# Two MLP pairs by whole products, token sums over both, and decoding that runs ahead and then rests

## The chip, the cores and the metric

The program runs on one core of a Trainium2 chip. The metric is the device time of one execution in microseconds (us); the time of before is the median of three runs. A core has TensorE (PE, the matrix products), VectorE (DVE), ScalarE (ACT), GpSimd (POOL) and SyncE (SP, which issues the transfers). Each takes its own instructions strictly in order; they wait for one another by semaphores.

## The reference, cut to what matters

```python
attn_out = attention(q, k, v, omega)          # linear attention over random features
x = attn_out.transpose(0, 2, 1, 3).reshape(2304, 512)
rms = sqrt(mean(x * x) + 1e-6);  xn = x / rms * rms_g
g = xn @ w_gate;  val = xn @ w_val            # GLU: 512 -> 1536
x = (g * sigmoid(g) * val) @ w_out            # 1536 -> 512
h = x @ w_in                                  # MLP: 512 -> 2048
out = (h * sigmoid(h)) @ w_out2               # 2048 -> 512
```

The weights are doubles (64 bit) in memory.

## The kernel before, in words

Attention comes first and fills about 180 us. The rest, of which the change is a part, is a stream of products over five blocks of tokens (0 to 3 of 512 tokens, 4 of 256). Each number is kept as a high and a low half (`xs` for tokens, `h` for hidden values, `w` for weights), and a product of two numbers is three matmuls (`PASS`, L191): 12 matmuls of 512 columns for one 128-wide slice of hidden features over one block (`part`, L205, or `product`, L513).

**GLU sweeps.** `groups` holds nine GLU groups of one slice (u = 0 to 8), then eight MLP groups of two slices each, a "pair" (u = 9 to 16). The first pair is `u == std` (9). Every group but `std` goes through `quad` (L520): blocks 0 and 1 against two weight matrices by seven half products of six matmuls in place of eight, which needs sums of token halves (`token_sums`, L344, L318 on POOL, halves by L327 and L330) and sums of weight halves (`sum12`, `sum34`, `shi`, `slo`). `std` alone uses whole products for blocks 0 and 1 (`g1_mlp`), since the token sums of the MLP's input don't exist yet. Blocks 2 to 4 are whole products everywhere.

**Second products.** `g2_glu` (L259) and `g2_mlp` (L292) multiply the hidden values by the output weights, tile by tile of 512 columns (a "y tile"), into one of four PSUM buffers `y`. In GLU sweeps DVE adds each tile to `ya` (L270); the buffer is free after that. Block 4's own first products use the same ring of four buffers. In the last GLU sweep (`done`) the sum is also the MLP's input: ACT writes its high half (L272) and DVE the low half (L249) into `xs`. So after the last sweep's first products come, in PE's order, y tiles of blocks 0 to 4 mixed with first products of blocks 3 and 4 and of `std` over blocks 0 and 1. This stretch is called the passage here.

**Decoding.** Every weight matrix comes as raw doubles by one transfer of SP, is decoded by five DVE operations (L146 to L157) and two POOL additions (L160), and split by ACT (high half, L411) and DVE (low half, L415). `WeightQueue` holds this as a list of jobs in a fixed order; each says how many free weight buffers it needs. The loop at the end of the kernel (L1484 to L1491) walks the stream, adds up the PE time of each piece in `due`, and lets one job be emitted whenever `due` exceeds `M_PACE` (2.0), unless `wq.hold` is set, as it is inside `quad`. A product that needs a weight emits the jobs up to it at once (`need`). Steps of the token sums (`sums`) are emitted by the same loop, one for each `T_PACE` (1.2) of PE time. The place at which a step is emitted is its place in its engine's order.

Of the kernel before, what the change touches and what calls it, by code (L numbers as in the profile page):

```python
# [20 lines left out]
def kernel(  # L21
# [168 lines left out]

    PASS = [(0, 0), (0, 1), (1, 0)]  # L191
    HALVES = [slice(0, 64), slice(64, P)]
    M_PACE, T_PACE = 2.0, 1.2
    W_EARLY, GRAIN, GATE = 3, 3, 3

    def split_h(s, j):
# [111 lines left out]

    KH = KC // 2
    tok, sums, ready = {}, [], set()  # L310
    std = next(u for u, g in enumerate(groups) if g[0] == 2)

    def w_tile(side, slot, dtype=F32R):
# [52 lines left out]

    class WeightQueue:
        def __init__(self):
            self.jobs, self.st, self.hold, self.free, self.held, self.tail = [], {}, True, [], {}, []
            for u in range(len(groups)):  # L370
                self.plan(u)

# [23 lines left out]
        def plan(self, u):  # L396
# [47 lines left out]
            load = self.load  # L444
            if kind == 1:
                jobs = [
                    (0, lambda: dec(a1, 1), lambda: load(u + 1, 1, 1)),
                    *self.tail,
                    (0, lambda: dec(a0, 0), lambda: load(u, bs[0], 0)),
# [8 lines left out]
                    (0, lambda: slo(1)),  # L458
                ]
                self.tail = [(1, lambda: hi(bs[0])), (0, lambda: lo(bs[0]))]  # L460
            elif u == std:
                jobs = [
                    *self.tail,
                    (0, lambda: dec(a1, 1), lambda: load(u, bs[1], 1)),
                    (0, lambda: dec(a0, 0), lambda: load(u, bs[0], 0)),
                    (0,),
                    (1, lambda: hi(a1)),
                    (1, lambda: lo(a1), lambda: hi(a0)),
                    (0, lambda: lo(a0), lambda: dec(bs[0], 0), lambda: load(u + 1, 0, 0)),
                    (0, lambda: dec(bs[1], 1), lambda: load(u + 1, 1, 1)),  # L470
                    (0,),
                    (1, lambda: hi(bs[0])),
                    (1, lambda: lo(bs[0]), lambda: hi(bs[1])),
                    (0, lambda: lo(bs[1])),
                ]
            else:
                jobs = [
                    (0, lambda: dec(a0, 0)),
                    (0, lambda: dec(a1, 1), lambda: load(u, bs[0], 0)),
                    (1, lambda: hi(a0), lambda: load(u, bs[1], 1)),  # L480
                    (1, lambda: lo(a0), lambda: hi(a1)),
                    (0, lambda: lo(a1), sum12),
                    (0, sum34),
                    (1, lambda: shi(0)),
                    (0, lambda: slo(0)),
                    (1, lambda: shi(1), lambda: dec(bs[0], 0)),
                    (0, lambda: slo(1), lambda: load(u + 1, 0, 0)),
                    (1, lambda: hi(bs[0]), lambda: dec(bs[1], 1)),
                    (0, lambda: lo(bs[0]), lambda: load(u + 1, 1, 1)),
                    (1, lambda: hi(bs[1])),  # L490
                    (0, lambda: lo(bs[1])),
                ]
# [143 lines left out]
    def stream():  # L636
# [25 lines left out]
        for u, (kind, fs) in enumerate(groups):  # L662
            first, last = kind == 2 and fs[0] == 0, u == len(groups) - 1
            done = u + 1 == std
            hs = {j: {} for j in range(NB)}
            if u == std:
                out_of = lambda j: g2_mlp(fs, j, hs[j], True, False, False)
                ys = iter(pend)
                now, later = token_sums(
                    lambda k: w_tile(1, 7, F32) if k == 2 else wq.slot(("t", k), F32),  # L670
                    lambda n: wq.release(("t", 1 - n)),
                )
                yield from g1_mlp(fs[0], 0, hs[0], (), take(ys, 4))
                yield from g1_mlp(fs[1], 0, hs[0], (), take(ys, 4))
                sums.extend(now)
                yield from g1_mlp(fs[0], 1, hs[1], (), ys)
                wq.release(*wq.keys(u - 1)[1])
                yield from g1_mlp(fs[1], 1, hs[1], (), out_of(0))
                sums.extend(later)
                yield from g1_mlp(fs[0], 2, hs[2], (), out_of(1))  # L680
                yield from g1_mlp(fs[1], 2, hs[2], (), ())
            else:
                yield from quad(u, iter(pend), hs)
            if u == std:
                pass
            elif u:
                wq.release(*wq.keys(u - 1)[1])
            else:
                wq.free += spent
# [9 lines left out]
                wq.release(*wq.keys(u)[0])  # L699
            else:  # L700
                out_of = lambda j, end=False: g2_mlp(fs, j, hs[j], first, last, end)
                if u != std:
                    for n, f in enumerate(fs):
                        yield from g1_mlp(f, 2, hs[2], (), out_of(1 - n))
                if last:
# [709 lines left out]
    with tc.manual_schedule():  # L1415
# [50 lines left out]
        n = 0  # L1466
# [13 lines left out]
        pools["w"][1] = late  # L1480
        pools["h"] = (late, 4)
        pools["s"] = (late, 3)
        due = 0.0
        for c in stream():  # L1484
            due += c
            if sums and due > T_PACE:
                sums.pop(0)()
                if wq.hold:
                    due = 0.0
            if due > M_PACE and not wq.hold and (wq.tick() or sums):  # L1490
                due = min(due - M_PACE, M_PACE)  # L1491


# [28 lines left out]
```

## Time and profile before

| | |
|---|---|
| median of 3 runs | 984.78 us (983.47 to 986.15) |
| profiled execution | 984.44 us, its span 982.7 us |
| PE busy | 949.7 us, 97% of the span |
| DVE, ACT, POOL busy | 699.1, 433.6, 416.5 us |
| mean granted TensorE clock | 0.991 of full speed |

Busy time of PE is of matmuls that overlap each other, so it reads as full wherever matmuls follow each other without a gap. The profile's slices show it full in nearly every slice; what it isn't full in lies at the start, near 220 us, and between 550 and 625 us. The last of these is the passage.

### The profile page before, as it was taken

Reading aid. Unit: us, or ns where it says so; the run is one execution under the profiler, and the core shown is the slowest. Engines: PE = TensorE matmul, PEld = TensorE weight load, DVE = VectorE, ACT = ScalarE, POOL = GpSimd, SP = SyncE. Lnnn points to the kernel's source line nnn. Section 1 sums busy time; section 2 is a strip of 40 time slices with the busy share of each in tenths; the row PEclk is TensorE's granted clock in tenths of the full one; section 3 lists DMA queues with packets and bytes.
Section 4 is the critical chain, followed back from the end, with each engine's and each line's share of the span. In section 5 each row is a group of like instructions: output and inputs, shape, how many; then the busy total and the mean of one; then the engine's idle time right before and its main releaser. Section 6 shows DMA issues by size and latency. Waiting matters only on the chain.

```text
span 982.7 us, 17038 instructions
## 1 busy us (share of the span) xinstructions
PE 949.7 (97%) x6564; PEld 794.2 (81%) x6564; DVE 699.1 (71%) x1372; ACT 433.6 (44%) x983; POOL 416.5 (42%) x406
## 2 busy tenths in 40 slices
PE   8999999998999999999999777999999999999998
PEld 6888878877888888888888655888888888888887
DVE  6998999656677677776767787648576757676653
ACT  6999886523433333333333234543242333333321
POOL 8887744315435335435533533324243333424200
PEclk9999999999999999999999989999999999999999
DMA  7654543012111112012011220002020211111023
GB/s 192 164 144 126 140 128 89 1 43 65 43 43 44 44 43 64 23 43 65 25 42 42 65 65 0 24 22 85 13 74 22 65 32 54 44 44 43 1 75 118
DMA packets 79489, 60.42 MB, mean 61 GB/s; under 512 B 27312, under 2 KB 73648, under 8 KB 79408
## 3 DMA queue, kind: packets, MB, share of 16 engines
q1 hardware_dynamic: 79136, 59.26, 20.8%
q8 instruction: 52, 0.85, 0.4%
q14 instruction: 29, 0.24, 0.1%
q10 hardware_dynamic: 272, 0.07, 0.0%
HBM read 49.87 MB, written 4.72 MB: 56 GB/s over the span
## 4 chain that ended last, share of the span: by engine, by line
PE 86%; DVE 7%; ACT 2%; DMA 2%; POOL 2%; issue 1%; SPq 1%; DVEq 0%; POOLq 0%
PE g L205 20%; PE y L292 20%; PE g L513 16%; PE y L259 12%; PE y L205 5%; PE b L992 3%; PE b L205 2%; PE b L1392 2%; PE kv L1072 2%; PE b L1176 2%; PE b L965 1%; DVE xs L249 1%; DVE ya L270 1%; POOL m L160 1%; PE b L1152 1%
## 5 line engine op out<-in xcount | busy, mean ns | idle before, releaser
L160 POOL TENSOR_TENSOR m<-m,raw 128x512 int32<-128x512 int32 x136 | 204.9, 1509 | 341.2 <-issue 193.5
L205 PE MATMUL g<-xs,w 128*128 128x512 f32 x1008 | 245.9, 391 | 0.0
L205 PEld LDWEIGHTS g<-xs,w 128*128 128x128 f32 x1008 | 189.9, 189 | 39.4
L292 PE MATMUL y<-w,h 128*128 128x512 f32 (+1 forms) x870 | 209.1, 390 | 3.9 <-ACT h L198 2.8
L292 PEld LDWEIGHTS y<-w,h 128*128 128x128 f32 x870 | 163.4, 189 | 38.9 <-ACT h L198 3.2
L259 PE MATMUL y<-h,w 128*128 128x512 f32 (+1 forms) x648 | 158.7, 371 | 15.2 <-DVE ya L270 9.8
L199 DVE TENSOR_TENSOR h<-s,h 128x512 fp32r<-128x512 f32 (+1 forms) x134 | 101.1, 759 | 95.0 <-ACT h L198 94.2
L270 DVE TENSOR_TENSOR ya<-y,ya 128x512 f32<-128x512 f32 (+1 forms) x200 | 123.0, 631 | 34.4 <-PE y L259 34.3
L259 PEld LDWEIGHTS y<-h,w 128*128 128x128 f32 x648 | 114.2, 190 | 38.4 <-DVE ya L270 10.4
L303 DVE TENSOR_TENSOR ya<-y,ya 128x512 f32<-128x512 f32 (+1 forms) x127 | 84.3, 679 | 56.9 <-PE y L292 56.3
L198 ACT ACTIVATE h<-s 128x512 fp32r<-128x512 f32 (+1 forms) x134 | 77.0, 585 | 100.6 <-DVE s L616 46.6
L513 PE MATMUL g<-xs,w 128*128 128x512 f32 x384 | 97.8, 390 | 0.0
L411 ACT ACTIVATE w<-m 128x512 fp32r<-128x512 f32 x75 | 47.1, 628 | 86.5 <-POOL m L160 73.9
L513 PEld LDWEIGHTS g<-xs,w 128*128 128x128 f32 x384 | 71.5, 188 | 14.8
L1041 ACT ACTIVATE e<-b,nb 128x128 f32<-128x128 f32 x272 | 76.1, 425 | 7.5 <-issue 4.3
L415 DVE TENSOR_TENSOR w<-m,w 128x512 fp32r<-128x512 f32 x66 | 59.6, 902 | 22.6 <-ACT w L411 22.6
L513 PE MATMUL g<-w,w 128*128 128x512 f32 x288 | 73.3, 390 | 0.0
L205 PEld LDWEIGHTS y<-xs,w 128*128 128x128 f32 x480 | 61.6, 191 | 8.2 <-DVE ya L270 6.1
L205 PE MATMUL y<-xs,w 128*128 128x256 f32 x480 | 62.7, 283 | 5.2 <-DVE ya L270 5.2
L513 PEld LDWEIGHTS g<-w,w 128*128 128x128 f32 x288 | 53.5, 188 | 10.7
L1009 DVE TENSOR_REDUCE small<-b 128x4 f32<-128x512 f32 (+1 forms) x80 | 51.3, 642 | 6.4 <-PE b L992 2.9
L536 ACT ACTIVATE s<-s 128x512 f32<-128x512 f32 x23 | 14.5, 632 | 80.1 <-DVE s L541 80.1
(119 smaller groups left out, 1165.2 us busy)
## 6 DMA issues: line engine op xcount, KB each, us to landing
raw<-in_moe_w_out_dram SPq DMA_DIRECT2D x28, 512.0 KB, 3.6
raw<-in_moe_w_in_dram SPq DMA_DIRECT2D x16, 512.0 KB, 3.6
raw<-in_moe_w_gate_dram SPq DMA_DIRECT2D x12, 512.0 KB, 3.5
raw<-in_moe_w_val_dram SPq DMA_DIRECT2D x12, 512.0 KB, 3.5
qT<-e SPq DMA_DIRECT2D x72, 64.0 KB, 2.3
x<-in_k_dram SPq DMA_DIRECT2D x16, 256.0 KB, 3.5
x<-in_q_dram SPq DMA_DIRECT2D x16, 256.0 KB, 3.0
va<-in_v_dram SPq DMA_DIRECT2D x32, 128.0 KB, 3.9
```

What stands on the lines that cost most here:

```text
L160: tt(out=mi, in0=mi, in1=(low if step == 5 else high).bitcast(I32), op=ALU.add)
L198: nc.scalar.activation(out=ht[:, 0, :], in_=s, func=AF.Copy)
L199: nc.vector.tensor_tensor(out=ht[:, 1, :], in0=s, in1=ht[:, 0, :].bitcast(F32), op=ALU.subtract)
L205: nc.tensor.matmul(out=ps, lhsT=w[:, a, cc * P:(cc + 1) * P], rhs=xs[j][:, c, cc, :], start=(n == 0), stop=(n == 3 * KC - 1),)
L259: nc.tensor.matmul(out=ps, lhsT=wt[1, "o", f][:, a, d * P:(d + 1) * P], rhs=hs[f][:, c, :], start=(n == 0), stop=(n == nn - 1),)
L270: nc.vector.tensor_tensor(out=y[:, d, :], in0=ps, in1=y[:, d, :], op=ALU.add)
L292: nc.tensor.matmul(out=ps, lhsT=hs[f][:, a, t * P:(t + 1) * P], rhs=wt[2, "p", f][:, c, d0:d1], start=(n == 0), stop=(n == nn - 1),)
L303: nc.vector.tensor_tensor(out=o[:, t, d0:d1], in0=ps, in1=o[:, t, d0:d1], op=ALU.add)
L415: eng.tensor_tensor(out=v[:, 1, :], in0=x, in1=v[:, 0, :].bitcast(F32), op=ALU.subtract)
L513: nc.tensor.matmul(out=ps, lhsT=w[:, a, (c0 + c) * P:(c0 + c + 1) * P], rhs=x(b, c), start=(start and n == 0), stop=(n == 3 * KH - 1), ski ...
L1009: nc.vector.tensor_reduce(out=st.mx.rearrange("p (j e) -> p e j", e=2)[:, e], in_=st.ps[e], axis=AX.X, op=ALU.max)
L1041: nc.scalar.activation(out=st.e[r][:, :, h, :] if blocks4 else st.e[r][:, h, :], in_=src.rearrange("p (a f) -> p a f", a=4) if blocks4 els ...
```

## The change

Four things change.

1. The first two pairs (`NSTD = 2`, u = 9 and 10) use whole products for blocks 0 and 1. The jobs of both have no weight sums any more.
2. The token sums start after `std`'s four products over blocks 0 and 1 (before: after the two over block 0), and their last two steps come in the second pair. A new counter `gone` spaces them: `T_PACE` while decoding rests, `M_PACE + T_PACE` otherwise.
3. In the last four GLU sweeps (u = 5 to 8) a job is emitted for every `A_PACE` = 1.6 of PE time and not 2.0. The first sweep gets one empty job ahead.
4. At the start of `std` `wq.hold` is set, and cleared after its fourth product over blocks 0 and 1 and the y tiles of block 0. While it is set, `due` is capped at `M_PACE`.

```diff
-    M_PACE, T_PACE = 2.0, 1.2
+    M_PACE, A_PACE, T_PACE = 2.0, 1.6, 1.2
...
+    NSTD = 2
...
             if kind == 1:
                 jobs = [
+                    *[(0,)] * (u == 0),
...
-            elif u == std:
+            elif std <= u < std + NSTD:
                 jobs = [
+                    (0, lambda: dec(a1, 1), lambda: load(u, bs[1], 1)),
                     *self.tail,
-                    (0, lambda: dec(a1, 1), lambda: load(u, bs[1], 1)),
                     (0, lambda: dec(a0, 0), lambda: load(u, bs[0], 0)),
-                    (0,),
                     (1, lambda: hi(a1)),
-                    (1, lambda: lo(a1), lambda: hi(a0)),
-                    (0, lambda: lo(a0), lambda: dec(bs[0], 0), lambda: load(u + 1, 0, 0)),
+                    (0, lambda: lo(a1)),
                     (0, lambda: dec(bs[1], 1), lambda: load(u + 1, 1, 1)),
+                    (1, lambda: hi(a0)),
+                    (0, lambda: lo(a0)),
+                    (0, lambda: dec(bs[0], 0), lambda: load(u + 1, 0, 0)),
...
+            wq.pace = A_PACE if std - 4 <= u < std else M_PACE
             hs = {j: {} for j in range(NB)}
-            if u == std:
+            if std <= u < std + NSTD:
...
+                wq.hold = first
                 yield from g1_mlp(fs[0], 0, hs[0], (), take(ys, 4))
                 yield from g1_mlp(fs[1], 0, hs[0], (), take(ys, 4))
-                sums.extend(now)
                 yield from g1_mlp(fs[0], 1, hs[1], (), ys)
                 wq.release(*wq.keys(u - 1)[1])
                 yield from g1_mlp(fs[1], 1, hs[1], (), out_of(0))
-                sums.extend(later)
+                wq.hold = False
+                if first:
...
+                    sums.extend(now)
+                if u == std + NSTD - 1:
+                    sums.extend(later)
                 yield from g1_mlp(fs[0], 2, hs[2], (), out_of(1))
...
-        due = 0.0
+        due = gone = 0.0
         for c in stream():
             due += c
-            if sums and due > T_PACE:
+            gone += c
+            if sums and gone > (T_PACE if wq.hold else M_PACE + T_PACE):
                 sums.pop(0)()
-                if wq.hold:
-                    due = 0.0
-            if due > M_PACE and not wq.hold and (wq.tick() or sums):
-                due = min(due - M_PACE, M_PACE)
+                gone = 0.0
+            if wq.hold:
+                due = min(due, M_PACE)
+            elif due > wq.pace and wq.tick():
+                due = min(due - wq.pace, wq.pace)
```

Three places show what moves. Names: `ya_95` to `ya_97`, `ya_3689` and `ya_3690` are the sums of blocks 0 to 4, `xs_90` to `xs_94` the tokens of blocks 0 to 4; line numbers after L310 are higher by one to five in the changed kernel.

First, DVE at the head of the passage, from the last `h` of the quad to the first y tile of block 0. Before:

```order
L146 TENSOR_SCALAR m_6849<-raw_6434 128x512
L149 TENSOR_SCALAR raw_6434<-raw_6434 128x512
L152 TENSOR_SCALAR m_6849<-m_6849 128x512
L154 TENSOR_SCALAR raw_6434<-raw_6434 128x512
L157 TENSOR_SCALAR m_6849<-m_6849 128x512
L146 TENSOR_SCALAR m_6860<-raw_6659 128x512
L149 TENSOR_SCALAR raw_6659<-raw_6659 128x512
L152 TENSOR_SCALAR m_6860<-m_6860 128x512
L154 TENSOR_SCALAR raw_6659<-raw_6659 128x512
L157 TENSOR_SCALAR m_6860<-m_6860 128x512
L270 TENSOR_TENSOR ya_95<-y,ya_95 128x512
```

The same place now, one row further on:

```order
L146 TENSOR_SCALAR m_6885<-raw_6685 128x512
L149 TENSOR_SCALAR raw_6685<-raw_6685 128x512
L152 TENSOR_SCALAR m_6885<-m_6885 128x512
L154 TENSOR_SCALAR raw_6685<-raw_6685 128x512
L157 TENSOR_SCALAR m_6885<-m_6885 128x512
L416 TENSOR_TENSOR w_0_6896<-m_6726,w_0_6896 128x512
L270 TENSOR_TENSOR ya_95<-y,ya_95 128x512
L621 TENSOR_TENSOR s<-s,g 128x512
L270 TENSOR_TENSOR ya_95<-y,ya_95 128x512
L249 TENSOR_TENSOR xs_90<-ya_95,xs_90 128x512
L416 TENSOR_TENSOR w_3_6926<-m_6885,w_3_6926 128x512
```

Two decodings stood ahead of the first L270 of `ya_95`; now one does, and the low half of a weight decoded earlier (L416). Further on, two decodings stand between the y tiles of block 0 in both kernels.

Second, DVE in the middle of the passage, from the last low half of block 1's tokens (`xs_91`) to the y tiles of block 2. Before:

```order
L249 TENSOR_TENSOR xs_91<-ya_96,xs_91 128x512
L146 TENSOR_SCALAR m_7054<-raw_6929 128x512
L149 TENSOR_SCALAR raw_6929<-raw_6929 128x512
L152 TENSOR_SCALAR m_7054<-m_7054 128x512
L154 TENSOR_SCALAR raw_6929<-raw_6929 128x512
L157 TENSOR_SCALAR m_7054<-m_7054 128x512
L270 TENSOR_TENSOR ya_97<-y,ya_97 128x512
L146 TENSOR_SCALAR m_7080<-raw_6952 128x512
L149 TENSOR_SCALAR raw_6952<-raw_6952 128x512
L152 TENSOR_SCALAR m_7080<-m_7080 128x512
L154 TENSOR_SCALAR raw_6952<-raw_6952 128x512
L157 TENSOR_SCALAR m_7080<-m_7080 128x512
```

The same place now:

```order
L249 TENSOR_TENSOR xs_91<-ya_96,xs_91 128x512
L199 TENSOR_TENSOR h<-s,h 128x256
L249 TENSOR_TENSOR xs_91<-ya_96,xs_91 128x512
L270 TENSOR_TENSOR ya_97<-y,ya_97 128x512 x2
L249 TENSOR_TENSOR xs_92<-ya_97,xs_92 128x512
L270 TENSOR_TENSOR ya_97<-y,ya_97 128x512
L249 TENSOR_TENSOR xs_92<-ya_97,xs_92 128x512
L270 TENSOR_TENSOR ya_97<-y,ya_97 128x512
L249 TENSOR_TENSOR xs_92<-ya_97,xs_92 128x512
L199 TENSOR_TENSOR h<-s,h 128x512
L249 TENSOR_TENSOR xs_92<-ya_97,xs_92 128x512
L270 TENSOR_TENSOR ya_3689<-y,ya_3689 128x512 x2
```

Both decodings are gone from here. One of them now stands between the y tiles of block 1, the others come after the passage.

Third, ACT behind the passage, after the last high half of block 4's tokens. Before:

```order
L239 ACTIVATE s<-g 128x512
L198 ACTIVATE h<-s 128x512
L411 ACTIVATE w_1_7228<-ws 128x512
L301 ACTIVATE ya_95<-y 128x512 x4
L327 ACTIVATE w_5_7279<-w_1_7174 128x1024
L239 ACTIVATE s<-g 128x512
L198 ACTIVATE h<-s 128x512
```

The same place now:

```order
L239 ACTIVATE s<-g 128x512
L198 ACTIVATE h<-s 128x512
L301 ACTIVATE ya_95<-y 128x512 x4
L239 ACTIVATE s<-g 128x512
L198 ACTIVATE h<-s 128x512
L301 ACTIVATE ya_96<-y 128x512
L412 ACTIVATE w_5_7310<-m_7026 128x512
L301 ACTIVATE ya_96<-y 128x512 x3
L239 ACTIVATE s<-g 128x512
L198 ACTIVATE h<-s 128x512
```

The high half of a token sum (L327 on `w_1`, which POOL makes) stood ahead of a silu (L239) and a high half of `h` (L198); now none stands there, and the four L327 come one by one from the start of the second pair on. On PE the second pair's seven groups of six matmuls over blocks 0 and 1 become four groups of twelve.

## Rows read from the trace of the kernel before

**Rows 1.** Windows of 25 us: PE, PEld, DVE, ACT, POOL busy; clock; DMA.

```profile
475.00:500.00 25.00, 25.00 (x123) 21.17 (x122) 18.21 (x35) 8.18 (x17) 14.41 (x12) 1.00 0.20 62
...
550.00:575.00 25.00, 16.68 (x75) 13.61 (x74) 21.37 (x33) 9.12 (x17) 9.24 (x7) 0.86 0.27 84
```

**Rows 2.** Lines of PE from 545.8 to 636.1, shapes apart: busy, mean | idle before.

```profile
L205 PE MATMUL g<-xs,w 128*128 128x512 f32 x127 | 32.8, 406 | 0.0
L292 PE MATMUL y<-w,h 128*128 128x512 f32 x72 | 19.1, 420 | 3.9 <-ACT h L198 2.8 <-DVE ya L270 1.1
L259 PE MATMUL y<-h,w 128*128 128x512 f32 x48 | 14.1, 414 | 6.6 <-DVE ya L270 6.6
L205 PE MATMUL y<-xs,w 128*128 128x256 f32 x48 | 7.5, 318 | 5.2 <-DVE ya L270 5.2
L259 PE MATMUL y<-h,w 128*128 128x256 f32 x12 | 2.4, 314 | 3.2 <-DVE ya L270 3.2
```

**Rows 3.** Chain that ended last, in order of time: start, us, what.

```profile
619.79 5.44 PE g L205 x24
...
633.39 2.83 PE y L205 x24
```

**Rows 4.** Timeline of PE in the passage: start, us, what [idle before].

```profile
556.01 0.84 PE L259 MATMUL y<-h,w 128*128 128x512 f32 x3
559.40 1.63 PE L205 MATMUL y<-xs,w 128*128 128x256 f32 x12 [2.54 <-DVE ya L270]
564.15 0.97 PE L259 MATMUL y<-h,w 128*128 128x512 f32 x3 [3.12 <-DVE ya L270]
567.77 2.93 PE L205 MATMUL y<-xs,w 128*128 128x256 f32 x12 [2.65 <-DVE ya L270]
...
595.49 4.51 PE L205 MATMUL g<-xs,w 128*128 128x512 f32 x12
...
603.92 3.02 PE L292 MATMUL y<-w,h 128*128 128x512 f32 x12 [1.14 <-DVE ya L270]
...
613.13 6.66 PE L292 MATMUL y<-w,h 128*128 128x512 f32 x21 [2.79 <-ACT h L198]
```

**Rows 5.** Timeline of DVE in the passage.

```profile
544.52 0.42 DVE L146 TENSOR_SCALAR m<-raw 128x512 uint32<-128x512 uint32 x1
...
547.88 0.68 DVE L270 TENSOR_TENSOR ya<-y,ya 128x512 f32<-128x512 f32 x1
551.20 1.13 DVE L415 TENSOR_TENSOR w<-m,w 128x512 fp32r<-128x512 f32 x1 [2.65 <-ACT w L411]
...
556.98 0.43 DVE L146 TENSOR_SCALAR m<-raw 128x512 uint32<-128x512 uint32 x1 [0.45 <-DMA raw<-in_moe_w_out_dram]
...
558.66 0.69 DVE L270 TENSOR_TENSOR ya<-y,ya 128x512 f32<-128x512 f32 x1
559.26 1.47 DVE L249 TENSOR_TENSOR xs<-ya,xs 128x512 fp32r<-128x512 f32 x1
560.65 1.50 DVE L146 TENSOR_SCALAR m<-raw 128x512 uint32<-128x512 uint32 x1
...
564.02 3.09 DVE L249 TENSOR_TENSOR xs<-ya,xs 128x512 fp32r<-128x512 f32 x2
...
597.43 1.22 DVE L344 TENSOR_TENSOR w<-xs 128x1024 f32<-128x1024 f32 x1
```

**Rows 6.** Timeline of POOL in the passage.

```profile
546.41 7.08 POOL L160 TENSOR_TENSOR m<-m,raw 128x512 int32<-128x512 int32 x4 [4.53 <-issue]
558.88 2.99 POOL L160 TENSOR_TENSOR m<-m,raw 128x512 int32<-128x512 int32 x2 [5.38 <-DVE m L157]
...
608.13 5.13 POOL L318 TENSOR_TENSOR w<-w,w 128x1024 f32<-128x1024 f32 x2 [4.89 <-DVE w L344]
```

**Rows 7.** Timeline of ACT behind the passage.

```profile
610.87 1.06 ACT L327 ACTIVATE w<-w 128x1024 fp32r<-128x1024 f32 x1 [2.27 <-POOL w L318]
```

**Rows 8.** Waits of PE, whole run: us, times, longest.

```profile
PE y L259 <- ACT h L198: 5.4, 1, 5.4
```

More of the change, by code (lines that the diff above doesn't have):

```diff
@@ L368, in __init__ @@
         def __init__(self):
-            self.jobs, self.st, self.hold, self.free, self.held, self.tail = [], {}, True, [], {}, []
+            self.jobs, self.st, self.hold, self.free, self.held, self.tail, self.pace = [], {}, True, [], {}, [], A_PACE
             for u in range(len(groups)):
@@ L460, in plan @@
                 self.tail = [(1, lambda: hi(bs[0])), (0, lambda: lo(bs[0]))]
-            elif u == std:
+            elif std <= u < std + NSTD:
                 jobs = [
+                    (0, lambda: dec(a1, 1), lambda: load(u, bs[1], 1)),
                     *self.tail,
-                    (0, lambda: dec(a1, 1), lambda: load(u, bs[1], 1)),
                     (0, lambda: dec(a0, 0), lambda: load(u, bs[0], 0)),
-                    (0,),
                     (1, lambda: hi(a1)),
-                    (1, lambda: lo(a1), lambda: hi(a0)),
-                    (0, lambda: lo(a0), lambda: dec(bs[0], 0), lambda: load(u + 1, 0, 0)),
+                    (0, lambda: lo(a1)),
                     (0, lambda: dec(bs[1], 1), lambda: load(u + 1, 1, 1)),
+                    (1, lambda: hi(a0)),
+                    (0, lambda: lo(a0)),
+                    (0, lambda: dec(bs[0], 0), lambda: load(u + 1, 0, 0)),
+                    (1, lambda: hi(bs[1])),
+                    (0, lambda: lo(bs[1])),
                     (0,),
                     (1, lambda: hi(bs[0])),
-                    (1, lambda: lo(bs[0]), lambda: hi(bs[1])),
-                    (0, lambda: lo(bs[1])),
+                    (0, lambda: lo(bs[0])),
                 ]
+                self.tail = []
             else:
@@ L664, in stream @@
             done = u + 1 == std
+            wq.pace = A_PACE if std - 4 <= u < std else M_PACE
             hs = {j: {} for j in range(NB)}
-            if u == std:
-                out_of = lambda j: g2_mlp(fs, j, hs[j], True, False, False)
+            if std <= u < std + NSTD:
+                out_of = lambda j: g2_mlp(fs, j, hs[j], first, False, False)
                 ys = iter(pend)
[L669 to L672, printed above, removed]
+                wq.hold = first
                 yield from g1_mlp(fs[0], 0, hs[0], (), take(ys, 4))
                 yield from g1_mlp(fs[1], 0, hs[0], (), take(ys, 4))
-                sums.extend(now)
                 yield from g1_mlp(fs[0], 1, hs[1], (), ys)
@@ L678, in stream @@
                 yield from g1_mlp(fs[1], 1, hs[1], (), out_of(0))
-                sums.extend(later)
+                wq.hold = False
+                if first:
+                    now, later = token_sums(
+                        lambda k: w_tile(1, 7, F32) if k == 2 else wq.slot(("t", k), F32),
+                        lambda n: wq.release(("t", 1 - n)),
+                    )
+                    sums.extend(now)
+                if u == std + NSTD - 1:
+                    sums.extend(later)
                 yield from g1_mlp(fs[0], 2, hs[2], (), out_of(1))
@@ L683, in stream @@
                 yield from quad(u, iter(pend), hs)
-            if u == std:
+            if std <= u < std + NSTD:
                 pass
@@ L701, in stream @@
                 out_of = lambda j, end=False: g2_mlp(fs, j, hs[j], first, last, end)
-                if u != std:
+                if u >= std + NSTD:
                     for n, f in enumerate(fs):
```

## The prediction

> **What bounds the kernel now.** I read the page's slices first, then windows of 25 us, then PE's own waits and the timelines of the passage. PE carries the kernel: from the first GLU sweep to the last pair it is full nearly everywhere, and DVE beside it is busy 18.21 us of 25 [rows 1]. The passage is the exception. From 550 to 575 us PE is busy 16.68 of 25, at a mean granted clock of 0.86, while DVE is busy 21.37 [rows 1]; the next 50 us look alike. What ended PE's idle time there is almost always DVE's addition of a y tile (L270) [rows 2]: PE waits for a `y` buffer, and DVE is late.
>
> What is the passage worth? From 545.8 to the second pair's first product at 636.1 are 90.3 us. In them stand 246 matmuls of 512 columns (126 of L205, 72 of L292, 48 of L259; the row's 127 holds one that began before) and 60 of 256 columns [rows 2]. Undisturbed, 24 of the first take 5.44 us and 24 of the second 2.83 [rows 3], so 227 and 118 ns each: 55.8 + 7.1 = 62.9 us. **Lost are 27.4 us.** Of these 18.9 are idle time (6.6 + 5.2 + 3.2 + 1.1 + 2.8 [rows 2]); the other 8.5 are matmuls that ran slower after a wait, as the 12 that took 4.51 and not 2.72, or the 21 that took 6.66 and not 4.76 [rows 4]. The mean clock below 1.00 [rows 1] is TensorE at 1.2 instead of 2.4 GHz for part of it.
>
> What makes DVE late? A decoding costs it 1.68 us (556.98 to 558.66 [rows 5]), if POOL lets it be. Its two POOL additions take 2.99 us [rows 6], and while they run DVE's next operations on SBUF alone are held: L249 took 1.39 instead of 0.60 (559.26 to 560.65), L146 1.43 instead of 0.34, two L249 3.02 instead of 1.20 [rows 5]. So a decoding can cost DVE 1.68 + 1.8 us. In the passage stand the 32 operations that nothing spares (16 L270 and 16 L249 of blocks 0 to 3, 0.6 each) and, besides, from 544.5 on, six decodings and three subtractions of token halves (L344, 1.2 each [rows 5]).
>
> **The change part by part.**
>
> *The second pair.* Seven half products of six matmuls become four whole ones of twelve: 48 and not 42, six more at 227 ns [rows 3], **+1.4 us** on PE, which is full there. Gone are four POOL sums, two ACT and two DVE halves of weights; they ran beside a full PE, so they give back nothing.
>
> *The passage.* I work through DVE's queue in its new order, with the prices above, on the clock of the trace. DVE is free at 544.5 [rows 5], and PE's order up to here is the old one. One decoding (to 546.2), the low half of a weight held by POOL (1.05, as at 551.20 [rows 5], to 547.3), first tile of block 0 (547.9), a GLU product, second tile (549.3), low half of the first, low half of a weight, low half of `h` (551.7, after ACT), a decoding (553.4), third tile: evacuated at 554.0, where before it was at 559.3 (558.66 + 0.69 [rows 5]). PE needs that buffer at 556.7 (behind the tile of 556.01 [rows 4]), so **the wait of 2.54 goes**. Then L249 held (1.39), a decoding whose first operation is held (2.77), fourth tile at 558.8: PE wants it at 558.1 and waits 0.7, not 3.12. Two L249 held (3.02), fifth tile at 562.4: PE wants it at 559.5 and **waits 2.9**, as it did 2.65. The third decoding comes among block 1's tiles: PE waits 0.3 ahead of it, and 1.2 behind it for the buffer of block 4's second product. From here on no decoding and no L344 is left in DVE's row, which goes at 0.6 a step; PE waits once more, 0.9, at block 4's last tile for the buffer of block 3's last. Together 0.7 + 2.9 + 0.3 + 1.2 + 0.9 = **6.0 us idle instead of 15.0 up to the product at 595.49** (18.9 less 1.14 and 2.79 [rows 4]).
>
> *Behind the passage.* The wait of 1.14 goes with the backlog. The one of 2.79 was ACT's: its L327 stood until 610.87 for POOL's subtraction [rows 7], with `h` (L198) behind it. Now no L327 is queued there: zero. What is late next? The token sums' new places: in the first pair 10 us of PE work lie between the L344 and the L327 that needs it, against 1.2 + 2.6 for an L344 and a subtraction (5.13 for two [rows 6]). In the second pair one place is tight: an L344, a subtraction and two weight sums stand ahead of a high half on ACT that was queued 3 us earlier, and a silu and an `h` of block 1 behind it. PE needs that `h` only 8 us on (24 matmuls of block 0's tiles, 12 of block 2: 36 x 0.227), so some 5 us are left. I take zero; the upper end is the slower rival.
>
> *Slow matmuls.* Before, 8.5 us for 18.9 idle, 0.45 for each. 6.0 x 0.45 = 2.7. Lost now: 8.7 of 27.4, **-18.7 us**.
>
> *The faster pace.* In the last four GLU sweeps as many decodings stand as before but for one more, so DVE's 18.2 of 25 [rows 1] rises by one decoding in some 180 us; they only stand closer. Four `y` buffers there are 8 us of PE work (24 + 12 matmuls, 36 x 0.227). I take zero; had PE to wait once in every sweep as it did at 602.8 (1.14 [rows 4]), it would be +4.6, a bound from above; below nothing is excluded, since PE has no wait to lose there.
>
> *The first sweep.* The one long wait outside, 5.4 us [rows 8], stands where two decodings precede a GLU product on DVE. Both are still there, with an L270 (0.6) between them: 0, within 0.6 either way.
>
> *Waiting of the queue.* The hold delays the second pair's decodings by some 25 us of PE time, yet its first weights are split by then, and its output weights stand 16 us of PE work ahead of their use. Zero.
>
> Sum against the profiled execution, 984.44 us (1.74 of it outside the span; the median of the runs is 984.78): 984.44 + 1.4 - 18.7 = **967.1 us**.
>
> **Here a rule is weighed.** While POOL's first addition came second, DVE's ten decoding operations went on at 0.34 (544.52 to 547.88 [rows 5]) and POOL's four took 7.08 instead of 5.98 [rows 6]; where POOL came first DVE was held [rows 5]. The Trainium skill (SBUF — State Buffer, Who interferes with whom) says that the two share a port pair, and that the one that issues first keeps it for the whole instruction while the other blocks; an operation with at most one SBUF input and outside the two-port modes is left alone. By that rule, if DVE came first each time, the sum would be that of the first rival; if POOL does, that of the forecast. The trace shows both orders.
>
> **The rivals.**
>
> *The passage is covered whole.* DVE isn't held in the new order. Then 0.45 + 0.8 + 1.1 + 1.8 = 4.2 us of held time go from the account above, the fifth tile is out at 558.2, ahead of 559.5, and the rest of the waits dissolve too: 984.44 + 1.4 - 27.4 = **958.4 us**. Against it: behind each decoding comes an L270, which reads PSUM and leaves POOL the first word, as at 558.66 [rows 5, 6].
>
> *Half of the wait stays.* The first three waits (2.54 + 3.12 + 2.65 = 8.3 [rows 4]) end where two decodings still stand; a later landing of raw weights (DVE stood for one at 556.98 [rows 5]) could keep them whole, and block 1 to 3 half of theirs, 6.7 / 2 = 3.3. Lost: 11.6 x 1.45 = 16.8, so 984.44 + 1.4 - 10.6 = **975.2 us**.
>
> *Slower: ACT stands behind POOL.* Each of four L327 and one high half of a weight sum now waits in the first two pairs for POOL, with silu and `h` of that pair queued behind. If each cost what the one at 610.87 did, 2.8 of wait and 1.9 of slow matmuls (6.66 - 4.76 [rows 4]), that is five times 4.7: 967.1 + 23.5 = **990.6 us**. It decides where POOL is more than the 5 us above behind, not at one place but at most of them; one such wait alone leaves the kernel faster.
>
> *The change does not do what it says.* The backlog is of L249 and L270 alone, and only the six matmuls show: **985.8 us**. Against it stand the held operations of rows 5.
>
> **How the numbers follow.** Forecast, 962.5 to 972: 0.68. Covered whole: 0.10. Half stays: 0.15. Slower: 0.04. Nothing but six matmuls: 0.03. Leaving out the last two, the lower edge of the first rival and the upper edge of the second, eight in ten lie in 960.5 to 975. About 0.3% (3 us) is what a measurement of this kernel tells from no change; faster holds the first three cases, 0.93; within 0.3% the last, 0.03; slower 0.04.
>
> **What would show it.** In the new trace: the first wait at an xs4 product gone, one wait near 2.9 us two y buffers later, no wait of PE on `h` in `std`, the stretch of the old 90.3 us some 19 shorter, the second pair 1.4 longer at full PE. Wrong would be PE idle over 10 us in the passage, a wait of PE in the last four GLU sweeps, or ACT waiting for POOL ahead of an L198 that PE then waits for.

## The result and the profile after

The changed kernel takes **974.91 us** (median of 4 runs, 973.74 to 975.15) where the kernel before, on the same chip, takes 984.88 (983.47 to 986.15): a ratio of 0.9897 [0.988, 0.9914], 10 us faster. That is 7.8 us above the predicted 967.1. It lies 0.1 us inside the upper edge of 960.5 to 975, where the prediction put eight in ten, but outside 962.5 to 972, the forecast proper; by the number alone it is the rival by which half of the wait stays (975.2). The profiled execution took 974.8 us, its span 972.9 against 982.7.

Windows of the kernel after, in the columns of [rows 1]:

```profile
450.00:475.00 25.00, 23.59 (x121) 19.76 (x120) 19.42 (x39) 7.45 (x16) 11.94 (x10) 1.00 0.21 64
475.00:500.00 25.00, 25.00 (x123) 21.05 (x122) 21.38 (x40) 10.96 (x26) 13.29 (x11) 1.00 0.17 46
500.00:525.00 25.00, 25.00 (x120) 20.98 (x119) 19.50 (x33) 7.08 (x13) 11.94 (x11) 1.00 0.12 39
525.00:550.00 25.00, 23.21 (x117) 19.34 (x116) 20.48 (x38) 6.96 (x13) 8.49 (x6) 1.00 0.20 64
550.00:575.00 25.00, 21.58 (x99) 18.03 (x98) 23.80 (x42) 8.38 (x15) 11.15 (x8) 0.93 0.21 64
```

The passage is what it was meant to become: PE is busy 21.58 us of 25 in place of 16.68, at a mean clock of 0.93 in place of 0.86. But two windows ahead of it, where PE used to be full, now have holes (23.59 and 23.21), and DVE, at 18.21 us from 475 to 500 [rows 1], is at 21.38 in the same window and near 20 beside it. The waits of PE from 450 to 690 us say what the holes are (engine, line, what was waited for: us in all, times, longest):

```profile
PE y L259 <- DVE ya L270: 3.3, 4, 1.3
PE y L205 <- DVE ya L270: 2.7, 1, 2.7
PE g L518 <- ACT g L529: 1.9, 2, 1.4
PE y L292 <- DVE h L199: 1.3, 1, 1.3
PE y L259 <- DVE s L621: 0.4, 1, 0.4
PE y L292 <- DVE ya L270: 0.2, 1, 0.2
```

Three kinds are new: `g` from ACT's copy (L529), `h` from DVE's low half (L199), and a short one for DVE's product in block 4 (L621). The wait for `h` from ACT of [rows 4] is gone.

To place gains and losses I cut the run at block 4's GLU or MLP product, the only ones of 256 columns on L205, which come at the same point of PE's order in each kernel. Four of them in PE's timeline after (the starts count; the numbers of matmuls and their times are cut at the edge of the window asked for):

```profile
451.47 1.58 PE L205 MATMUL y<-xs,w 128*128 128x256 f32 x12
...
562.50 0.75 PE L205 MATMUL y<-xs,w 128*128 128x256 f32 x5
...
621.11 2.05 PE L205 MATMUL y<-xs,w 128*128 128x256 f32 x16
...
671.85 1.34 PE L205 MATMUL y<-xs,w 128*128 128x256 f32 x10
```

Before, the same products began at 449.79, 559.40 [rows 4], 633.23 and 680.97. The stretches between them, and one earlier (**entry**, from the first such product, at 188.29 before and 188.45 after, to the last ahead of the first sweep's half products, at 239.63 and 241.30), for both kernels and for the experiments that follow, in us:

| kernel | entry | last sweeps | passage and first pair | second pair | ratio to before |
|---|---|---|---|---|---|
| before | 51.34 | 109.61 | 73.83 | 47.74 | 1 |
| after | 52.85 | 111.03 | 58.61 | 50.74 | 0.9897 |
| e1_pace2 | 52.91 | 106.90 | 66.76 | 50.76 | 0.9927 |
| e2_pace18 | 51.94 | 106.90 | 58.14 | 50.76 | 0.9841 |
| e3_sweep1 | 53.23 | 106.90 | 57.12 | 50.76 | 0.9844 |
| e4_thin | 52.20 | 106.90 | 54.76 | 49.10 | 0.9790 |
| e5_second | 52.62 | 106.93 | 59.24 | 49.11 | 0.9822 |
| e6_spread | 51.90 | 106.92 | 57.37 | 49.11 | 0.9805 |
| e7_nohold | 52.28 | 111.05 | 60.82 | 50.74 | 0.9895 |
| e8_onepair | 52.54 | 111.01 | 57.12 | 66.15 | 1.0033 |
| e9_onepair_sums | 52.47 | 111.02 | 57.35 | 52.93 | 0.9893 |
| e10_three | 52.17 | 106.92 | 54.99 | 49.10 | 0.9794 |
| e11_phase | 51.94 | 107.02 | 57.15 | 49.11 | 0.9825 |

An undisturbed stretch of last sweeps is 106.9 (three sweeps of 35.63); before's 109.61 holds the passage's first wait of 2.54. So the changed kernel lost 4.1 us in the sweeps. From 545.81 (before) and 551.62 (after), where block 0's tiles begin, to the product at 633.23 and 621.11 it won 87.42 - 69.49 = **17.9 us**. The second pair is 3.0 longer, the entry 1.5; everywhere else the kernels run alike within 0.2 us up to 947, and 0.6 is won at the very end.

### The profile page after: what moved, and what is told of

It is laid out like the page before. It is cut to its first block, busy times and chain, and to the rows that moved or that the text cites. A ratio compares the mean times of both kernels' runs of the same rounds, so it can differ in the third digit from the quotient of the medians.

```text
span 972.9 us, 17023 instructions
## 1 busy us (share of the span) xinstructions
PE 949.4 (98%) x6570; PEld 793.6 (82%) x6570; DVE 698.6 (72%) x1368; ACT 431.5 (44%) x978; POOL 416.7 (43%) x402
## 5 line engine op out<-in xcount | busy, mean ns | idle before, releaser
L160 POOL TENSOR_TENSOR m<-m,raw 128x512 int32<-128x512 int32 x136 | 208.2, 1533 | 332.4 <-DVE m L157 169.4
L205 PE MATMUL g<-xs,w 128*128 128x512 f32 x1056 | 255.5, 390 | 0.0
L205 PEld LDWEIGHTS g<-xs,w 128*128 128x128 f32 x1056 | 197.7, 188 | 40.8
L292 PE MATMUL y<-w,h 128*128 128x512 f32 (+1 forms) x870 | 206.6, 388 | 1.5 <-DVE h L199 1.3
L292 PEld LDWEIGHTS y<-w,h 128*128 128x128 f32 x870 | 162.3, 188 | 35.8 <-DVE h L199 1.8
L199 DVE TENSOR_TENSOR h<-s,h 128x512 fp32r<-128x512 f32 (+1 forms) x134 | 101.1, 760 | 74.9 <-ACT h L198 74.1
L270 DVE TENSOR_TENSOR ya<-y,ya 128x512 f32<-128x512 f32 (+1 forms) x200 | 123.4, 632 | 25.5 <-PE y L259 25.4
L303 DVE TENSOR_TENSOR ya<-y,ya 128x512 f32<-128x512 f32 (+1 forms) x127 | 84.8, 681 | 62.9 <-PE y L292 62.3
L198 ACT ACTIVATE h<-s 128x512 fp32r<-128x512 f32 (+1 forms) x134 | 77.0, 585 | 118.6 <-DVE s L621 60.7
L518 PE MATMUL g<-xs,w 128*128 128x512 f32 x360 | 91.7, 390 | 0.0
L416 DVE TENSOR_TENSOR w<-m,w 128x512 fp32r<-128x512 f32 x65 | 60.4, 930 | 29.6 <-ACT w L412 29.3
L518 PEld LDWEIGHTS g<-xs,w 128*128 128x128 f32 x360 | 67.1, 188 | 13.9
L518 PE MATMUL g<-w,w 128*128 128x512 f32 x270 | 69.1, 391 | 1.9 <-ACT g L529 1.9
L205 PEld LDWEIGHTS y<-xs,w 128*128 128x128 f32 x480 | 61.7, 191 | 5.3 <-DVE ya L270 3.1
L205 PE MATMUL y<-xs,w 128*128 128x256 f32 x480 | 62.6, 283 | 2.7 <-DVE ya L270 2.7
L518 PEld LDWEIGHTS g<-w,w 128*128 128x128 f32 x270 | 49.9, 188 | 12.8 <-ACT g L529 2.8
L1019 DVE TENSOR_REDUCE small<-b 128x4 f32<-128x512 f32 (+1 forms) x80 | 51.3, 642 | 6.3 <-PE b L1002 2.9
```

What stands on the lines that cost most here:

```text
L160: tt(out=mi, in0=mi, in1=(low if step == 5 else high).bitcast(I32), op=ALU.add)
L198: nc.scalar.activation(out=ht[:, 0, :], in_=s, func=AF.Copy)
L199: nc.vector.tensor_tensor(out=ht[:, 1, :], in0=s, in1=ht[:, 0, :].bitcast(F32), op=ALU.subtract)
L205: nc.tensor.matmul(out=ps, lhsT=w[:, a, cc * P:(cc + 1) * P], rhs=xs[j][:, c, cc, :], start=(n == 0), stop=(n == 3 * KC - 1),)
L270: nc.vector.tensor_tensor(out=y[:, d, :], in0=ps, in1=y[:, d, :], op=ALU.add)
L292: nc.tensor.matmul(out=ps, lhsT=hs[f][:, a, t * P:(t + 1) * P], rhs=wt[2, "p", f][:, c, d0:d1], start=(n == 0), stop=(n == nn - 1),)
```

## The experiments

My theory after the result: the passage's account is right; the pace costs 4.1 us because decodings stand close together; one decoding costs the second pair 1.6; the edits of the first sweep cost 1.5; behind the first two stand POOL's additions, which hold DVE. The rivals are named with each run. All ratios are to the kernel before on the same chip, with 95% intervals of 0.0012 to 0.0024 either way.

### The pace

**e1_pace2** takes the faster pace back, alone.

```
-            wq.pace = A_PACE if std - 4 <= u < std else M_PACE
+            wq.pace = M_PACE
```

> The faster pace is undone (a decoding each 2.0 us of PE work in every sweep); the hold, the second pair and the first sweep stay as changed. Theory: the pace costs 4.1 us ahead of the passage (the three PE waits of 1.41, 1.26 and 0.53 us at 461, 529 and 535 us and the slow matmuls behind them), so these waits go and block 4's last products before the passage begin 3.5 to 4 us earlier. The decodings that no longer fit ahead now stand in the end of the first pair, beside the additions of token halves, where DVE has 0.6 us of work for each product: up to 2 us lost there. Together 971 to 973 us. Rival: the pace is what the passage lives on; DVE is late in the first pair by as much as was won, and the time is 975 us or more.

979.85 us, 0.9927. The theory is right on the sweeps (106.90, all three waits gone) and wrong on the sum: passage and first pair together lose 8.2 us, and the rival wins. The passage itself wins: from block 4's product to the first pair's first tile (L292) are 27.67 us (560.35 to 588.02) and 31.33 in the changed kernel (562.50 to 593.83). The first pair behind that tile loses 11.8. Four decodings now stand there, and PE waits for what DVE has last in its row:

```profile
591.54 8.33 PE L292 MATMUL y<-w,h 128*128 128x512 f32 x23 [3.12 <-DVE w L416]
...
618.60 5.95 PE L292 MATMUL y<-w,h 128*128 128x512 f32 x19 [3.33 <-DVE h L199]
```

The matmuls behind the first took 8.33 us for 23 where 24 take 5.60 undisturbed. So the faster pace costs 4.1 us in the sweeps and 3.7 in the passage, and saves 11.8 in the first pair.

**e2_pace18** sets it halfway, for the last four sweeps alone (the queue's first pace is kept at 1.6).

```
-    M_PACE, A_PACE, T_PACE = 2.0, 1.6, 1.2
+    M_PACE, A_PACE, T_PACE = 2.0, 1.8, 1.2
```

> The pace of the last four sweeps is 1.8 us of PE work for a job and not 1.6: three decodings in a sweep and not four in the last two, and in the passage four as before but standing in two twos. Theory (the pace costs by the number of decodings that stand close together in a sweep): the waits of 1.41, 1.26 and 0.53 us go, 4 us are won ahead of the passage, the passage idles 5 to 8 us in place of 5.4; 971 to 973 us. Rival (only where a decoding stands matters, not how many): waits appear at other places of the same size, 974 to 977 us.

971.1 us, 0.9841, as the theory has it: 106.90 in the sweeps, and the passage idles 2.65 for block 4's GLU product on DVE (L621) and 1.8 elsewhere, less than the 5 to 8 expected. But with their number the decodings' places changed too, so this run alone doesn't tell the two apart. **e3_sweep1**, made for another question, does.

```
-                    *[(0,)] * (u == 0),
...
-            [...] self.pace = [], {}, True, [], {}, [], A_PACE
+            [...] self.pace = [], {}, True, [], {}, [], M_PACE
```

> The two edits of the first sweep are undone (no empty job ahead of its first, the old pace before it). Theory: the 1.5 us lost between 224 and 240 us come from DVE's order there, so the product that began at 241.3 begins at 239.6 to 239.9 again and the wait at 224 is 5.4 and not 5.66 us. Rival: the wait and the slow matmuls behind it scatter by themselves, and the 1.5 us stay or come at another size. All later jobs move by a part of a us of PE work, so the waits of the last sweeps may differ; the total lies between 971 and 977 us, 973.4 if nothing else changes.

971.68 us, 0.9844. The entry did *not* come back: the old order there gives 53.23, the longest of all, and the wait is 5.78. The old order stands in three kernels (before, e3, e11: 51.34, 53.23 and 51.94), the new one in the others (51.90 to 52.91). The rival holds: no effect of the edit stands out of the scatter. What won is a thing that I had only called "may differ": all later jobs moved against PE's work. By how much is not shown; the rows below show one that fell behind a low half and a tile. Counted from block 4's product at 451.47, DVE begins nine decodings within 81 us in the changed kernel, and nine in e3_sweep1 and in e11_phase at nearly the same pace; there PE waits for none of them (106.90 and 107.02). The first begins 4.5 us behind the product in the changed kernel and 4.9 in the two others, the eighth at 74.5 (72.7 without the first wait) and at 73.7 and 74.6. **The pace costs by where a decoding falls, not by its number.** DVE's timeline shows the first place, in the changed kernel:

```profile
455.97 0.43 DVE L146 TENSOR_SCALAR m<-raw 128x512 uint32<-128x512 uint32 x1 [1.73 <-POOL w L416]
...
457.65 0.69 DVE L199 TENSOR_TENSOR h<-s,h 128x512 fp32r<-128x512 f32 x1
458.25 0.69 DVE L270 TENSOR_TENSOR ya<-y,ya 128x512 f32<-128x512 f32 x1
458.85 1.20 DVE L416 TENSOR_TENSOR w<-m,w 128x512 fp32r<-128x512 f32 x1
459.98 0.41 DVE L621 TENSOR_TENSOR s<-s,y 128x256 f32<-128x256 f32 x1
```

then ACT's and PE's, at the same time:

```profile
460.42 0.42 ACT L198 ACTIVATE h<-s 128x256 fp32r<-128x256 f32 x1 [5.07 <-DVE s L621]
460.74 0.58 ACT L529 ACTIVATE g<-g 128x512 f32<-128x512 f32 x1
```

```profile
457.06 0.84 PE L259 MATMUL y<-h,w 128*128 128x512 f32 x3
...
461.37 1.66 PE L518 MATMUL g<-w,w 128*128 128x512 f32 x6 [1.41 <-ACT g L529]
```

DVE's product of block 4 (L621) stands behind a decoding, a low half, a y tile and a low half of a weight held by POOL; ACT stands 5.07 us for it, with the copy of `g` (L529) queued behind, whose product was done by 457.2; PE has 2.9 us of work before it needs that copy (six matmuls and two tiles, 457.06 to 459.96). In e3_sweep1 the low half and the tile come ahead of the decoding, the product of block 4 (L620 there) directly behind it and the held L416 only after that (458.93, 460.61 and 462.95, in a profile that runs 2.5 us later), and the copy is in time.

### What POOL's additions cost

**e4_thin** leaves every operation of DVE and shortens POOL's.

```
+        elif step < 7 and thin:
+            mf = st.m.bitcast(F32)[:, 0:8]
+            tt(out=mf, in0=mf, in1=(low if step == 5 else high).bitcast(F32)[:, 0:8], op=ALU.add)
         elif step < 7:
```

> In the decodings of the last four GLU sweeps and of the first two MLP pairs POOL's two additions work on 8 of 512 columns (as float additions, and without the shift ahead of them), so the weights are not those of the reference; all of DVE's operations stay, in number, size and order. Theory (POOL's additions hold DVE): the held operations return to 0.34 and 0.6 us, and the waits of the changed kernel that stand behind them (1.41, 1.26, 2.71 and 1.32 us, with the slow matmuls behind them) go: 8 to 11 us less, 964 to 967 us. Rival (DVE's own five operations of a decoding are too much in one place): the waits stay but for a third, 971 us or more.

965.76 us, 0.979 [0.9769, 0.9812]: 4.1 us less in the sweeps, 3.9 in the passage, 1.6 in the second pair, 9.6 together. The theory's waits are gone; those that stay (0.67, 0.78 and 0.58) stand where no operation of DVE is held. The same three operations of the second pair, behind the same decoding, in the kernel after (lines L199, L416) and in this one (L202, L421):

```profile
660.55 1.77 DVE L199 TENSOR_TENSOR h<-s,h 128x512 fp32r<-128x512 f32 x1 [0.23 <-ACT h L198]
662.25 1.79 DVE L416 TENSOR_TENSOR w<-m,w 128x512 fp32r<-128x512 f32 x1
663.96 1.28 DVE L199 TENSOR_TENSOR h<-s,h 128x512 fp32r<-128x512 f32 x2
```

```profile
652.23 0.69 DVE L202 TENSOR_TENSOR h<-s,h 128x512 fp32r<-128x512 f32 x1 [0.23 <-ACT h L201]
652.84 0.69 DVE L421 TENSOR_TENSOR w<-m,w 128x512 fp32r<-128x512 f32 x1
653.46 0.68 DVE L202 TENSOR_TENSOR h<-s,h 128x512 fp32r<-128x512 f32 x1
```

1.08 and 1.10 us of each are hold. These stand in the same order in both, so the second pair's 1.6 are hold. In the sweeps the decodings also begin some 3 us sooner (DVE had stood 1.73 us for POOL ahead of the one at 455.97), and ACT gets its halves sooner, so there the 4.1 are hold and place together. In the passage the first decoding begins 1.29 us ahead of block 0's first tile in both, DVE's order is the same, and its 16 low halves of tokens (L249, L252 there) take 0.68 to 0.69 where four had been held, for up to 1.76; what is won there is hold, but for the scatter of the matmuls behind the waits.

### The second pair

**e5_second** queues the decoding of those rows earlier, with the pace of 1.8.

```
-                    (1, lambda: shi(1), lambda: dec(bs[0], 0)),
+                    *[(0, lambda: dec(bs[0], 0))] * (u == std + NSTD),
+                    (1, lambda: shi(1), *[lambda: dec(bs[0], 0)] * (u != std + NSTD)),
```

> The pace of 1.8 as in the run before, and in the second pair the one decoding that stands ahead of three halves of h (L199) is queued 5 us of PE work earlier, between the additions of block 1's tiles, where DVE idles 0.67 us a tile. Theory (POOL's two additions behind that decoding hold the L199 that PE waits for): the wait of 1.32 us at block 3's tiles in the second pair goes and nothing takes its place, 1.3 to 1.6 us less than the pace of 1.8 alone, so 0.9825 to 0.983 of the time of before, and 969.5 us where before has 987. Rival (DVE is full in the second pair wherever the decoding stands): the wait moves to a y buffer of block 1 or to the same h, and the time stays at 0.984 of before.

970.07 us, 0.9822. The wait (it stands at block 2's tiles, not block 3's as I had written) is gone: the second pair takes 49.11 in place of 50.76, and that is 47.74 + 1.37, the six matmuls and nothing else. In the changed kernel that decoding had stood behind a low half of the token sums (L331), which frees the weight buffer that its job needs; ACT's high half of the same job waited for it too:

```profile
657.43 1.22 DVE L331 TENSOR_TENSOR w<-w,w 128x1024 fp32r<-128x1024 f32 x1
658.56 0.42 DVE L146 TENSOR_SCALAR m<-raw 128x512 uint32<-128x512 uint32 x1
```

```profile
658.74 0.64 ACT L412 ACTIVATE w<-m 128x512 fp32r<-128x512 f32 x1 [9.81 <-DVE w L331]
```

In the passage, where its order is e2_pace18's, it took 1.1 longer: behind the same wait of 0.58 twelve matmuls that took 2.90 there took 4.24 here. So the ratio shows little of the 1.65.

**e8_onepair** and **e9_onepair_sums** undo the second pair's new form and put the token sums into the first pair, with two buffers kept free for them.

```
-    NSTD = 2
+    NSTD = 1
```

> Only the first pair by whole products; the second pair goes back to seven half products, and all token sums to the first pair, with pace and rest as changed. Theory (the passage's gain is the pace's and the rest's, and the second pair's form is a price for it): the passage keeps its 17.9 us of gain within 2 us, the second pair has six matmuls fewer (1.4 us), but its three weights are decoded within 5 us of PE work, at 3.4 us of DVE each against 1.7 to spare, which holds PE 2 to 5 us; 0.989 to 0.993 of before. Rival (the second pair's form gives the queue the room it needs): the first pair's end and the second pair lose 8 us or more, 0.997 of before or above.

990.55 us, 1.0033 [1.0021, 1.0046], slower than before. The passage kept its gain (57.12), but the second pair took 18.4 us longer than before. The largest wait is not for a decoding:

```profile
634.61 0.79 PE L521 MATMUL g<-xs,w 128*128 128x512 f32 x1 [8.54 <-ACT xs L328]
```

It is for a token half, at the end of a chain of sums that the changed kernel spaces by 3.2 us of PE work and that the first half product needs all at once. Two waits for weights, of 1.61 and 2.43 us, stand behind it; they are the 2 to 5 us that the theory had. e9 lets them follow each other after 1.2 us again.

```
-            if sums and gone > (T_PACE if wq.hold else M_PACE + T_PACE):
+            if sums and gone > T_PACE:
```

> As e8_onepair, but the token sums, which there stood in a heap at the end of the first pair because each waited for 3.2 us of PE work, follow each other after 1.2 us as in the kernel before, all within the first pair. Theory (e8's loss is the heap of token sums: 8.5 us of wait for L328 and what follows): 12 to 18 us of e8's 18 lost in the second pair come back, 0.985 to 0.991 of before, so the second pair by whole products is worth nothing by itself and is 1.4 us too long. Rival (the decodings of the second pair, three within 5 us of PE work, are the loss): waits of PE for w from L412 and L416 of 4 us and more stay, 0.994 or above.

975.95 us, 0.9893 [0.9869, 0.9916], the same as the changed kernel. Against it the first stretch is 1.3 shorter and the second 2.2 longer, with waits of 1.4 and 1.4 for token halves; the waits for weights are gone too. So in the changed kernel whole products in the second pair pay for their six matmuls, and no more; with token sums spaced wide they are needed. With the decoding moved as in e5_second the second pair takes 3.8 us less than e9's.

### The rest, and better places

**e7_nohold** lets the queue run through the passage; two buffers are kept free for the token sums here too.

```
-                wq.hold = first
+                wq.keep = 2 if first else 0
...
-            if self.jobs and self.jobs[0][0] <= len(self.free):
+            if self.jobs and self.jobs[0][0] and self.jobs[0][0] <= len(self.free) - self.keep or [...]
```

> The changed kernel without its rest: the queue goes on through the passage (two buffers are kept free for the token sums, which start at the same place as changed). The only decoding that moves is one of the second pair's, from the end of the first pair to block 2's tiles in the passage. Theory (what the passage gains is that few decodings stand in it; each costs 1.7 us of DVE and 1.4 of held operations): one or two waits of PE for a y buffer among block 2's tiles, 2 to 4 us together with slow matmuls, 0.992 to 0.994 of before. Rival (the backlog is worked off by then, and the rest is worth nothing): 0.990, as with the rest.

977.89 us, 0.9895 [0.9879, 0.9911]: the rival's number, and below the theory's range; by the whole time the rest is not shown to be worth anything. The profile began its sweeps 1.9 us earlier by chance; in it the passage is 2.2 longer, with two more waits (0.35 and 0.74) at block 3's tiles, not block 2's, behind the decoding that moved, and twelve slow matmuls ahead (3.85 us for 2.92). So the rest saves 1.1 us of idle time in this profile; that the other 1.1 are its own, one profile doesn't show.

**e6_spread** is e5_second with one empty job in the first pair's list, **e10_three** with two, so that one of the passage's four decodings falls behind the rest.

```
                     *self.tail,
+                    *[(0,)] * (u == std),          # e10_three: (2 * (u == std))
                     (0, lambda: dec(a0, 0), lambda: load(u, bs[0], 0)),
```

> As e5_second, with one empty job ahead of the second decoding of the first pair's weights: the passage's decodings stand at other places, two beside block 0's tiles 3 us of PE work apart and two beside block 1's, 3 us apart. Theory (PE waits only where two decodings and an L249 held by POOL come ahead of the operation that frees the buffer PE wants): the wait of 2.65 us on the GLU product of block 4 becomes under 1 us, 2 us less than e5_second. Rival (each decoding costs the passage the same wherever it stands): a wait of 2 to 3 us at another tile, the time within 1 us of e5_second.

968.39 us, 0.9805 [0.9791, 0.982]. The wait of 2.65 became one of 2.71 at block 3's first tile, behind the two decodings' new place: the rival, as far as the wait goes. The 1.9 us by which the passage is shorter than e5's are mostly e5's slow matmuls.

> As e6_spread with one more empty job: the passage has three decodings and not four (two 6 us of PE work apart, one behind block 1's tiles), the fourth goes to the first pair beside two others. Theory (a decoding less in the passage is a wait less): the wait of 2.71 us at block 2's tiles goes, the passage is 3 to 4 us shorter than e6's, the first pair loses 0 to 2; 0.977 to 0.979 of before. Rival (as with the pace undone, decodings in the end of the first pair hold the low half of h or a weight that PE waits for): a wait of 2 us or more there, 0.980 or above.

966.5 us, 0.9794 [0.9777, 0.9811], the lowest ratio here of a kernel that computes the reference (e6_spread's interval overlaps), 1.0% under the changed one by the two ratios. Passage and first pair take 54.99, as without long additions of POOL (54.76), and 2.4 less than e6's, where 3 to 4 were expected. The wait of 2.71 (at block 3's tiles) did not go but shrank to 1.37, the longest that is left:

```profile
563.54 1.68 PE L205 MATMUL y<-xs,w 128*128 128x256 f32 x12 [0.40 <-DVE ya L270]
...
576.83 0.96 PE L259 MATMUL y<-h,w 128*128 128x512 f32 x3 [1.37 <-DVE ya L270]
```

The decoding that left the passage costs nothing in the first pair (27.32 us from its first tile to block 4's product, 27.28 in the changed kernel), where DVE is busy 22.52 us of 25 and PE is full; e1 had four there, e10 three.

```profile
600.00:625.00 25.00, 25.00 (x123) 21.18 (x122) 22.52 (x24) 14.15 (x25) 17.88 (x9) 1.00 0.21 64
```

**e11_phase** is e5_second with the first sweep's old order, as in e3_sweep1, and another pace.

```
-    M_PACE, A_PACE, T_PACE = 2.0, 1.8, 1.2
+    M_PACE, A_PACE, T_PACE = 2.0, 1.65, 1.2
```

> Pace 1.65, no empty job in the first sweep, and the second pair's decoding queued early as in e5_second: four decodings in the next to last sweep and in the passage as changed, but 1 to 3 us of PE work later in each sweep. Theory (where a decoding stands decides, not how many): no PE wait in the last four sweeps, as in e3_sweep1, the passage's waits as there (2.6 and four under 0.8), no wait in the second pair; 0.981 to 0.983 of before. Rival (the faster pace costs by its number): the 4.1 us in the sweeps come back, 0.985 to 0.987.

969.4 us, 0.9825 [0.9805, 0.9845]: no PE wait in the sweeps, 2.62 once in the passage, none in the second pair (49.11). The theory's numbers.

## Why the prediction was right in the passage and 8 us short in the sum

- *The passage*, -18.7 forecast, -17.9 measured. The queue was worked through rightly: the wait of 2.54 is gone (the product at 562.50 waits for nothing), the next is 0.71 (0.7 forecast), the long one 2.71 two `y` buffers later (2.9). Then 0.43 behind the third decoding, for the buffer of block 4's second product (1.2, and 0.3 ahead of it), and 0.77, 0.58 and 0.18 at block 4's tiles and behind (0.9). Together 5.4 us idle for 6.0. No PE wait for `h` in `std`. The slow matmuls behind the waits cost more than I took: of the 72.3 us from block 0's tiles to the second pair, 62.9 are work and 5.4 idle, so some 4 us and not 2.7. Undoing the pace lost 8.2 of the 17.9, undoing the rest 2.2, undoing the second pair's form none; what the new order of jobs and the later token sums bring by themselves was not run.
- *The faster pace*, 0 forecast, **+4.1** measured, a term mis-sized. I took the four `y` buffers as the cover, and so 8 us. The waits that came (1.41 and 0.53, beside one of 1.26 for `y`) came through ACT: a slack of only 2.9 us between a product's end and the use of its copy, with a block's `h` queued ahead of the copy. The share of DVE in a window said nothing on it. The wait for `y` shows that the four buffers fell short too, at two decodings 4.3 us apart (521.64 and 525.93). The bound of 4.6 held, but it was priced on another wait. That a PE wait in these sweeps would show the forecast wrong was said, and it did.
- *The second pair*, +1.4 forecast, +3.0 measured. The six matmuls are 1.37 (e5). The tight place that I priced held: ACT stood 3.91 us for POOL's weight sum, and PE didn't wait. What I left out is that the last low half but one of the token sums frees a weight buffer, on which a decoding had waited, and that the decoding then stands directly ahead of the `h` that PE wants: 1.6 with slow matmuls.
- *The first sweep*, 0 within 0.6 forecast, +1.5 seen, and by e3 and e11 not shown to be the edit's: thirteen profiles scatter from 51.3 to 53.2.
- *The sum.* 0.2 ahead of the entry, then 1.5 + 4.1 - 17.9 + 3.0, and 0.6 won at the end, make the spans' -9.7. That the whole still lies inside the wide range, by 0.1 us, is near to luck: the pace's 4.1 and the second pair's 1.6 were not in the sum, and the entry's 1.5 are not shown to be the change's. Of the rivals none happened, though the number is that of the second: that one had 10.6 us won in the passage and a first wait that stays, and 17.9 were won and the wait of 2.54 went. The others fail too: ACT stood behind POOL without harm, and the passage was not covered whole (not even in e4, where DVE isn't held).
- *The rule that was weighed.* Without POOL's long additions DVE's operations behind these decodings return to 0.69. The Trainium skill (SBUF — State Buffer, Who interferes with whom) calls the shared port pair an exclusive lock; e4's rows agree. The rows of the changed kernel agree with the forecast that POOL comes first here: behind the second and third decoding L249, the next decoding's first operation and two L249 took 1.48, 1.52 and 3.14 us. Without the long additions passage and first pair are 3.9 us shorter.

## What to carry to other kernels

An engine's mean share in a window doesn't say what a moved step will cost: look for the operation with the least slack behind it, through every in-order queue it passes, and place the step just after that. Running ahead is paid where it is put: here the stretches became 9.4 us shorter by other places for decodings alone (e10_three), and 9.6 by cutting the helper engine's additions short (e4_thin). A wait that the whole time can't show is read from the distance between two fixed products.

## What the runs showed of the hardware

In the second pair each of POOL's two additions held one operation of DVE: 1.77 and 1.79 us in place of 0.69, in a row. DVE's additions of y tiles (L270), which read PSUM, were not held: from 420 to 680 us all 73 of 512 columns took 0.68 to 0.69, also at 564.06, with POOL's addition from 564.27 on. The PE wait at the entry was 5.4 to 5.9 us in all thirteen profiles, but the 12 matmuls behind it took from 4.65 to 5.79 us (2.88 undisturbed), in no relation to the order that I changed; the window from 225 to 250 us had a mean granted clock of 0.95 before, 0.89 after and 0.86 in e3_sweep1, TensorE at 1.2 in place of 2.4 GHz for part of it. And the product that opens the entry, up to which every kernel runs the same operations in the same order, began between 187.1 and 191.6 us. So some 2 us either way of any single profile are not the kernel's, and they hide effects like e7's in the whole time.
